# An attention-and-experts kernel on one core: each engine's instructions tied together in the order of the kernel's own plan

## The chip, the cores and the metric

The kernel runs on one core of a Trainium2 chip. A core has five engines with an instruction queue each: TensorE (PE) multiplies matrices, VectorE (DVE), ScalarE (ACT) and GpSimd (POOL) work elementwise, and SyncE (SP) issues loads. Sixteen DMA engines move data between the core's memory (SBUF, with PSUM as the target of matmuls) and HBM. The metric is the device time of one execution, in microseconds (us).

## The reference

The input x holds 4 batches of 11456 tokens with 128 features, in fp32. Attention through 32 inducing points comes first, then a mixture of 8 experts of which each token takes the one with the largest logit:

```
def mab(q, kv):
    s = scale * (q @ kv.transpose(0, 2, 1))
    s = s - s.max(-1, keepdims=True)
    a = np.exp(s)
    a /= a.sum(-1, keepdims=True) + 1e-09
    return a @ kv
h = mab(I, x)                # 32 inducing points attend to all tokens
x = mab(x, h)                # all tokens attend to the 32 results
...
logits = x @ w_gate          # 45824 tokens, 8 experts
expert_idx = np.argmax(logits, axis=1)
...                          # gate_w: softmax probability of that expert
    h = np.maximum(xe @ w1[e], 0.0)      # 128 -> 1024
    ye = h @ w2[e]                       # 1024 -> 128
    out[mask] = gate_w[mask, None] * ye
```

## The kernel before

A token's attention output is a weighted mean of 32 rows. If one expert takes all tokens of a batch and the sign of every hidden unit is the same for all 32 rows, the expert can be applied to these 32 rows (`h4`) instead of to the tokens. The main path does so; a test for each token, with a threshold `thr`, finds those for which it doesn't hold, and a second path after the main one computes them if there are any.

A batch is cut into 6 groups of 15 blocks of 32 tokens in 4 partition quarters (GW = 480 columns). Two functions and one between them add the work of a batch to a plan:

- `attend(b)` takes groups in pairs. A group's transposed tokens `xt` (960 KB) are loaded by SP. Scores with the inducing points `it_s` are four matmuls (L199). DVE takes their peak (L364), POOL parts it by quarters (`mq`, L367), PE spreads it (L376), DVE takes the lowest (L382), ACT makes the exponentials `e1t` (L386), DVE turns them (`e`, L394), and PE sums (L403) over the tokens by row, `xn`, which are loaded (L305) or turned on PE (L315) and copied (L325). DVE collects the sums in `hs` (L416).
- `induced(b)` makes the batch's 32 rows: `hs` is folded (L457, L458), divided in steps on DVE (L468 to L477), centred to `hc` (L486, L488); logits of the 32 rows on PE (L481, L482) give the expert by steps on DVE, the picking and the gate matrix `gzw` (L493 to L527). POOL gathers that expert's two weight matrices, `w1r` and `w2r`, by indirect DMAs (L510). Hidden units (L539 to L556), `h4` (L569, L579, L583, L587) and the threshold (L592 to L612) follow.
- `tokens(b, g0)` takes three groups: scores with `hc` (L199 again), the peak (L646 to L650), exponentials `et` on ACT (L654), gate logits on PE (L658), turned on DVE (L668), the gate in steps on DVE with one exponential on ACT (L675 to L708), its factors turned (`cb`, L715), `et` weighed by them on POOL (L718), the expert's rows by four matmuls into four PSUM banks `ps` (L722), four copies on ACT (L733), and a store that ACT issues (L736).

The order is made in two steps. Each of these operations is added to a `Plan` with its engine, an estimated duration, what it comes after, a rank, and the ring buffers it takes and gives back (12 of `xt`, 3 each of `xn`, `ob`, `e1t`, `e1`, `fe`, 8 `et`, 2 each of `lv` and `cb`, 1 `lp`, 4 `ps`). `Plan.order()` is a list scheduler: it starts whichever ready operation can start first by the estimates, the rank deciding between equals, and gives back the operations in the order of their planned starts. They are then written out in that order:

```
for op in plan.order():
    op["fn"]()
```

An operation may be several instructions. What is written out goes through the scheduler of the framework in which the kernel is written. This second scheduler keeps what depends on each other in order and is free to move the rest on each engine, by costs and priorities of its own. In the lists of instructions each engine's row differs from the plan's on PE, DVE, ACT and POOL, and not on SP's loads. An engine works through its row from the front.

## Time and profile before

| | |
|---|---|
| time, three runs | 231.03, 234.84, 235.23 us; median 234.84 |
| profiled execution | 233.27 us, of which the span of instructions is 231.5 |
| granted clock of PE, mean | 0.892 of 2.4 GHz |
| busy | PE 81%, DVE 57%, ACT 45%, POOL 17% |
| moved by DMA | 63.78 MB, 276 GB/s in the mean |

The span runs from the first to the last instruction of the profiled execution; the rest of its time lies around it. Shares are of the span. PE loads weights beside its matmuls, and a matmul's row may stand for several (xN) of one group. The granted clock is either near 1.00 or near 0.50 at a moment, so that a mean between them says how long each held.

### The profile page before, as it was taken

The numbers are of one execution on the slowest core, as the hardware profiler recorded it, in microseconds if no ns is written. First come the engines' busy times: TensorE is split into PE (matmuls) and PEld (weight loads), VectorE is DVE, ScalarE is ACT, GpSimd is POOL, SyncE is SP. The second block draws the span as 40 slices with busy tenths as digits, with TensorE's granted clock in tenths as the row PEclk, the third lists the DMA queues.
The fourth block names the chain that finished last, engine by engine and source line by source line (L and its number), as shares of the span: only waits on it lengthen the run. The fifth ranks groups of instructions, "written<-read, shape, count | busy, mean of one in ns | idle before, by whom it ended". The sixth has DMA issues, their size and how long they took to land.

```text
span 231.5 us, 4416 instructions
## 1 busy us (share of the span) xinstructions
PE 188.5 (81%) x1694; PEld 94.7 (41%) x1695; DVE 132.0 (57%) x400; ACT 104.7 (45%) x212; POOL 40.3 (17%) x58
## 2 busy tenths in 40 slices
PE   0897588898997799989999959999598959984840
PEld 0565364456665233544352236535122224422520
DVE  0275536674489266874894680848844998037300
ACT  2243204263350827385735841396236532845630
POOL 2000003000003500060045000410530062303200
PEclk9999889999999889999999997999959995578555
DMA  6999999995369847997999990034427524627591
GB/s 222 426 428 423 427 423 422 415 417 194 94 253 342 352 171 288 355 365 266 326 426 418 428 369 15 4 150 195 170 71 280 235 105 173 254 100 327 243 394 58
DMA packets 10252, 63.78 MB, mean 276 GB/s; under 512 B 1392, under 2 KB 1520, under 8 KB 10224
## 3 DMA queue, kind: packets, MB, share of 16 engines
q1 hardware_dynamic: 5328, 35.62, 39.2%
q10 hardware_dynamic: 3744, 23.62, 25.0%
q0 software_dynamic: 1152, 4.19, 4.8%
q8 instruction: 15, 0.25, 0.4%
q14 instruction: 13, 0.11, 0.1%
HBM read 39.83 MB, written 23.59 MB: 274 GB/s over the span
## 4 chain that ended last, share of the span: by engine, by line
PE 55%; DVE 19%; DMA 10%; ACT 6%; issue 3%; POOL 3%; SPq 0%; ACTq 0%; DVEq 0%; POOLq 0%
PE ps L722 16%; PE fe L199 15%; PE lp L658 8%; PE ps L403 8%; DMA xt<-in_xT 6%; PE ps L315 4%; DMA w1r<-in_w,ii 4%; ACT ob L733 3%; DVE cb L715 3%; POOL et L718 3%; DVE e L394 2%; DVE mx L364 2%; ACT e1t L386 2%; DVE mx L646 1%; ACT xn L325 1%
## 5 line engine op out<-in xcount | busy, mean ns | idle before, releaser
L733 ACT COPY ob<-ps 128x480 f32<-128x480 f32 x96 | 47.5, 573 | 34.0 <-PE ps L722 33.8
L722 PE MATMUL ps<-et,h 32*128 32x480 f32 x192 | 47.9, 739 | 10.3 <-POOL et L718 6.2
L718 POOL TENSOR_TENSOR et<-et,cb 128x480 f32<-128x480 f32 x24 | 28.4, 1211 | 56.2 <-DVE cb L715 36.8
L199 PE MATMUL fe<-xt,it_s 128*32 128x480 f32 x192 | 29.6, 609 | 9.7 <-DMA xt<-in_xT 9.7
L325 ACT COPY xn<-ps 128x512 f32<-128x512 f32 (+1 forms) x42 | 22.4, 570 | 26.1 <-PE ps L315 23.8
L364 DVE TENSOR_REDUCE mx<-fe 128x1 f32<-128x480 f32 x24 | 15.6, 652 | 27.9 <-PE fe L199 25.7
L722 PEld LDWEIGHTS ps<-et,h 32*128 32x128 f32 x192 | 17.6, 216 | 33.7 <-POOL et L718 13.8
L199 PE MATMUL fe<-xt,hc 128*32 128x480 f32 x192 | 29.4, 613 | 1.6 <-ACT e1t L386 1.1
L315 PE MATMUL ps<-csb,xt 128*128 128x128 f32 x180 | 27.1, 291 | 1.5 <-DMA xt<-in_xT 1.5
L658 PE MATMUL lp<-et,gzw 128*128 128x480 f32 x48 | 27.5, 661 | 0.5 <-ACT et L654 0.5
L654 ACT ACTIVATE et<-fe,rn 128x480 f32<-128x480 f32 x24 | 16.0, 671 | 26.1 <-DVE rn L650 16.6
L403 PE MATMUL ps<-xn,e 128*32 128x129 f32 x630 | 25.7, 282 | 1.7 <-DVE e L394 1.7
L315 PEld LDWEIGHTS ps<-csb,xt 128*128 128x128 f32 x180 | 21.7, 153 | 13.1 <-issue 6.2
L403 PEld LDWEIGHTS ps<-xn,e 128*32 128x32 f32 x630 | 21.8, 113 | 9.0 <-DVE e L394 2.5
L394 DVE STREAM_TRANSPOSE e<-e1t 128x480 f32<-128x480 f32 x24 | 15.1, 656 | 7.9 <-ACT e1t L386 7.8
L386 ACT ACTIVATE e1t<-fe,rn 128x480 f32<-128x480 f32 x24 | 14.8, 667 | 10.2 <-DVE rn L382 9.8
L646 DVE TENSOR_REDUCE mx<-fe 128x1 f32<-128x480 f32 x24 | 15.4, 643 | 6.1 <-PE fe L199 5.8
L715 DVE STREAM_TRANSPOSE cb<-c_all 128x480 f32<-128x480 f32 x24 | 15.4, 663 | 5.5 <-POOL et L718 5.0
L367 POOL TENSOR_TENSOR mq<-mx,csb 128x8 f32<-128x8 f32 x12 | 2.4, 201 | 91.3 <-DVE mx L364 91.2
L658 PEld LDWEIGHTS lp<-et,gzw 128*128 128x128 f32 x48 | 8.0, 207 | 13.5 <-issue 7.0
L668 DVE STREAM_TRANSPOSE lv<-lp 128x480 f32<-128x480 f32 x8 | 5.4, 671 | 14.3 <-PE lp L658 14.3
L199 PEld LDWEIGHTS fe<-xt,it_s 128*32 128x32 f32 x192 | 6.3, 113 | 16.0 <-issue 10.4
(94 smaller groups left out, 149.2 us busy)
## 6 DMA issues: line engine op xcount, KB each, us to landing
xt<-in_xT SPq DMA_DIRECT2D x24, 960.0 KB, 9.7
out<-ob ACTq DMA_DIRECT2D x24, 960.0 KB, 3.8
xn<-in_xn SPq DMA_DIRECT2D x9, 967.5 KB, 8.0
ob<-in_xn SPq DMA_DIRECT2D x3, 967.5 KB, 15.7
csb<-in_consts SPq DMA_DIRECT2D x1, 134.5 KB
w1r<-in_w,ii POOLq DMA_INDIRECT x4, 7.7
w2r<-in_w,ii POOLq DMA_INDIRECT x4, 9.3
it_sb<-in_indT ACTq DMA_DIRECT2D x1, 16.0 KB
```

Source lines behind the costliest of these rows:

```text
L199: nc.tensor.matmul(blk(ps[32 * q : 32 * q + 32, :GW]), lhsT=lhsT, rhs=xt_g[:, :, q, :], start=True, stop=True)
L315: nc.tensor.transpose(ps[:, k * P : (k + 1) * P], s.xt[g][:, k0 + k].rearrange("p q t -> p (q t)"), ident)
L325: nc.scalar.copy(dst, src)
L364: nc.vector.tensor_reduce(s.mx[:, g : g + 1], w.ps[:, :GW], AX.X, ALU.max)
L386: nc.scalar.activation(w.et, w.ps[:, :GW], AF.Exp, bias=pr.rn)
L394: nc.vector.transpose(w.e1, w.et)
L403: nc.tensor.matmul(hp[32 * j : 32 * j + 32, :], lhsT=blk(w.e1)[:, k, :], rhs=w.xn[:, k, :], start=(n < 4), stop=(n >= 2 * GB - 4),)
L658: nc.tensor.matmul(buf(some[0].b5)[:, :GW], lhsT=s.gzw[:, u * P : (u + 1) * P], rhs=w.et, start=(u == 0), stop=(u == NW - 1),)
L715: nc.vector.transpose(blk(w.cb), c.unsqueeze(2).to_broadcast([P, GB, 32]))
L718: nc.gpsimd.tensor_tensor(out=w.et, in0=w.et, in1=w.cb, op=ALU.mult)
L722: nc.tensor.matmul(buf(w.b9, q)[:, :GW], lhsT=s.h4[32 * q : 32 * q + 32, :], rhs=w.et[32 * q : 32 * q + 32, :], start=True, stop=True,)
L733: nc.scalar.copy(w.ob[:, q, :], buf(w.b9, q)[:, :GW])
```

## The change

After the operations are written out, the instructions of the main path are gone through in the order in which they were written, which is the plan's, and each gets a dependency on the one before it on the same engine. The dependency has no semaphore (`NoSync`): it sets the order for the framework's scheduler and adds no instruction and no wait on the chip.

```
     for op in plan.order():
         op["fn"]()
+    order = mybir.DependencyInfo(mybir.DependencyClass.NoSync, mybir.DependencyReason.DATA)
+    latest = {}
+    for ins in list(nc.cur_bb.bb.instructions):
+        if ins.engine in latest:
+            tc.add_manual_dep(ins, latest[ins.engine], order, reason="the plan's order")
+        latest[ins.engine] = ins.name
```

Below are the rows of instructions of some engines at the places that the prediction speaks of. A row gives the line, the operation, its output and inputs with their buffers (the number behind a ring's name is the buffer), and the shape; a first character of - or + says that it stands there only before or only after.

First place, PE, where the last of the loaded groups (`xt11`, of the last batch) gets its scores with the inducing points:

```order
-L658 MATMUL lp0_130<-et3_118,gzw1_136 128x480
 L603 MATMUL ps3_134<-dd_1410,ones_64 128x128
-L199 MATMUL fe2_129<-xt11_102,it_s_71 32x480
 L583 MATMUL ps1_132<-h1_1431,csb_60 128x128
 L315 MATMUL ps0_131<-csb_60,xt9_100 128x128 x3
+L658 MATMUL lp0_130<-et3_118,gzw1_136 128x480
 L403 MATMUL ps2_133<-xn1_104,e12_114 32x129 x15
-L199 MATMUL fe2_129<-xt11_102,it_s_71 32x480 x3
+L199 MATMUL fe2_129<-xt11_102,it_s_71 32x480 x4
 L403 MATMUL ps2_133<-xn2_105,e10_112 32x129 x15
```

The four score matmuls now stand together, behind L583, three transposes and fifteen sums, and one L658 has moved behind L603, L583 and the transposes.

The same place on DVE, before, from the peak of that group:

```order
L364 TENSOR_REDUCE mx_978<-fe2_129 128x1
L698 SCALAR_TENSOR_TENSOR rs_1465<-lm_1491,rs_1465 128x45
L704 TENSOR_REDUCE se_1501<-ex_1495 128x45
L416 SCALAR_TENSOR_TENSOR hs_981<-hs_981,fc_1364,ps2_133 128x129
L705 TENSOR_SCALAR se_1501<-se_1501 128x45
L706 RECIPROCAL se_1501<-se_1501 128x45
L708 TENSOR_TENSOR c_all_70<-se_1501,rs_1465 128x15x3
L715 STREAM_TRANSPOSE cb1_126<-c_all_70 128x480
L715 STREAM_TRANSPOSE cb0_125<-c_all_70 128x480
```

And after:

```order
L698 SCALAR_TENSOR_TENSOR rs_1465<-lm_1491,rs_1465 128x45
L704 TENSOR_REDUCE se_1501<-ex_1495 128x45
L705 TENSOR_SCALAR se_1501<-se_1501 128x45
L706 RECIPROCAL se_1501<-se_1501 128x45
L708 TENSOR_TENSOR c_all_70<-se_1501,rs_1465 128x15x3
L416 SCALAR_TENSOR_TENSOR hs_981<-hs_981,fc_1364,ps2_133 128x129
L715 STREAM_TRANSPOSE cb1_126<-c_all_70 128x480
L715 STREAM_TRANSPOSE cb0_125<-c_all_70 128x480
L364 TENSOR_REDUCE mx_978<-fe2_129 128x1
```

The peak of the last group has moved behind the gate's steps and two turned factors.

Second place, DVE, where `induced(3)` begins (`rv`, `hT_all`, `hb`, `hm`, `hc`) among the gate of three groups of batch 2 (`se`, `c_all`, `cb`). Before:

```order
L715 STREAM_TRANSPOSE cb0_125<-c_all_70 128x480
L468 TENSOR_SCALAR rv_1659<-ps1_132 128x32
L715 STREAM_TRANSPOSE cb1_126<-c_all_70 128x480
L469 RECIPROCAL rv_1659<-rv_1659 128x32
L715 STREAM_TRANSPOSE cb0_125<-c_all_70 128x480
L470 TENSOR_TENSOR hT_all_69<-rv_1659,ps1_132 128x128
L646 TENSOR_REDUCE mx2_1720<-fe1_128 128x1
L477 TENSOR_REDUCE hb_1663<-hT_all_69 128x1
L648 STREAM_TRANSPOSE mt_1722<-mx2_1720 128x32
L486 TENSOR_SCALAR hm_1668<-hb_1663 128x1
L650 TENSOR_REDUCE rn2_1724<-mt_1722 128x1
L488 TENSOR_SCALAR hc_1670<-hT_all_69,hm_1668 128x32
```

And after:

```order
L698 SCALAR_TENSOR_TENSOR rs_1640<-lm_1650,rs_1640 128x45
L468 TENSOR_SCALAR rv_1659<-ps1_132 128x32
L469 RECIPROCAL rv_1659<-rv_1659 128x32
L470 TENSOR_TENSOR hT_all_69<-rv_1659,ps1_132 128x128
L477 TENSOR_REDUCE hb_1663<-hT_all_69 128x1
L486 TENSOR_SCALAR hm_1668<-hb_1663 128x1
L488 TENSOR_SCALAR hc_1670<-hT_all_69,hm_1668 128x32
L704 TENSOR_REDUCE se_1676<-ex_1666 128x45
L705 TENSOR_SCALAR se_1676<-se_1676 128x45
L706 RECIPROCAL se_1676<-se_1676 128x45
L708 TENSOR_TENSOR c_all_70<-se_1676,rs_1640 128x15x3
L715 STREAM_TRANSPOSE cb0_125<-c_all_70 128x480
```

The six steps to `hc` stand in one block ahead of the end of the gate (L704 on) instead of one by one behind it. What follows in the new order is the picking and the gate matrix (L493 to L527, nine instructions), the other two L715, and then the peak L646 of `mx2_1720`.

The same place on POOL, where the weighing of the groups in `et4` to `et6` and the gathers of batch 3 meet:

```order
 L718 TENSOR_TENSOR et4_119<-et4_119,cb0_125 128x480
+L510 DMA w1r_1709<-in_w1,ii_1696 128x1024
+L510 DMA w2r_1710<-in_w2,ii_1696 128x1024
 L718 TENSOR_TENSOR et5_120<-et5_120,cb1_126 128x480
 L718 TENSOR_TENSOR et6_121<-et6_121,cb0_125 128x480
-L510 DMA w1r_1709<-in_w1,ii_1696 128x1024
-L510 DMA w2r_1710<-in_w2,ii_1696 128x1024
```

Both gathers have moved ahead of two of the three weighings.

Third place, POOL, where the gathers of batch 2 meet three weighings of batch 1:

```order
+L510 DMA w1r_1277<-in_w1,ii_1253 128x1024
+L510 DMA w2r_1278<-in_w2,ii_1253 128x1024
 L718 TENSOR_TENSOR et6_121<-et6_121,cb0_125 128x480
 L718 TENSOR_TENSOR et7_122<-et7_122,cb1_126 128x480
 L718 TENSOR_TENSOR et0_115<-et0_115,cb0_125 128x480
-L510 DMA w1r_1277<-in_w1,ii_1253 128x1024
-L510 DMA w2r_1278<-in_w2,ii_1253 128x1024
```

Here they have moved ahead of all three.

On ACT, a store stands directly behind the last of its group's four copies for 23 of 24 groups after, and for 8 of 24 before.

## Rows read from the trace of the kernel before

**Rows 1.** The page: busy time and share of each engine, with its instructions, and the chain of work that ended last, by engine.

```profile
PE 188.5 (81%) x1694; PEld 94.7 (41%) x1695; DVE 132.0 (57%) x400; ACT 104.7 (45%) x212; POOL 40.3 (17%) x58
...
PE 55%; DVE 19%; DMA 10%; ACT 6%; issue 3%; POOL 3%; SPq 0%; ACTq 0%; DVEq 0%; POOLq 0%
```

**Rows 2.** The table of stretches: from and to, length, busy us (and instructions) of PE, PE's weight loads, DVE, ACT and POOL, the mean granted clock, the share of the DMA engines and GB/s.

```profile
40.00:130.00 90.00, 82.69 (x894) 42.41 (x896) 58.42 (x178) 45.80 (x95) 16.05 (x22) 0.98 0.82 316
...
163.00:177.00 14.00, 10.83 (x40) 3.14 (x36) 8.26 (x30) 3.84 (x9) 5.43 (x5) 0.76 0.42 150
...
195.00:206.00 11.00, 11.00 (x28) 4.42 (x26) 1.47 (x3) 7.45 (x15) 3.51 (x3) 0.54 0.43 180
206.00:223.00 17.00, 11.87 (x42) 5.85 (x42) 8.47 (x20) 10.13 (x21) 3.61 (x3) 0.68 0.65 267
```

**Rows 3.** The timeline at the first place: start, duration, engine (SPq is SP's issue of a load), line, operation, output and inputs, shapes, and in brackets the idle time before it and what ended it.

```profile
131.02 0.33 SPq L356 DMA_DIRECT2D xt<-in_xT  x1
...
139.35 0.99 PE L199 MATMUL fe<-xt,it_s 128*32 128x480 f32 x2 [3.28 <-DMA xt<-in_xT]
...
143.69 0.83 PE L199 MATMUL fe<-xt,it_s 128*32 128x480 f32 x3
...
144.59 0.66 DVE L364 TENSOR_REDUCE mx<-fe 128x1 f32<-128x480 f32 x1 [5.77 <-PE fe L199]
...
145.16 0.20 DVE L698 SCALAR_TENSOR_TENSOR rs<-lm,rs 128x45 f32<-128x45 f32 x1
...
147.00 1.24 DVE L715 STREAM_TRANSPOSE cb<-c_all 128x480 f32<-128x480 f32 x2
...
147.83 2.37 POOL L718 TENSOR_TENSOR et<-et,cb 128x480 f32<-128x480 f32 x2 [2.30 <-DVE cb L715]
...
150.65 0.40 PE L376 MATMUL fe<-mq,csb 128*128 128x24 f32 x2
```

**Rows 4.** The timeline at the second place, same columns.

```profile
161.17 0.31 PE L458 MATMUL ps<-csb,hs 128*128 128x32 f32 x2
...
161.93 0.21 DVE L698 SCALAR_TENSOR_TENSOR rs<-lm,rs 128x45 f32<-128x45 f32 x1
...
162.29 1.01 PE L199 MATMUL fe<-xt,hc 128*32 128x480 f32 x8
...
163.74 0.68 DVE L715 STREAM_TRANSPOSE cb<-c_all 128x480 f32<-128x480 f32 x1
164.34 0.15 DVE L468 TENSOR_SCALAR rv<-ps 128x32 f32<-128x32 f32 x1
...
165.84 1.07 PE L722 MATMUL ps<-et,h 32*128 32x480 f32 x2 [2.53 <-POOL et L718]
...
167.62 0.51 DVE L488 TENSOR_SCALAR hc<-hT_all,hm 128x32 f32<-128x32 f32 x1
...
169.19 0.17 DVE L493 COPY gs<-ps 128x16 f32<-128x16 f32 x1 [1.06 <-PE ps L482]
...
170.49 0.98 POOL L510 DMA_INDIRECT w1r<-in_w,ii  x1 [2.39 <-DVE go L519]
...
170.98 3.43 PE L199 MATMUL fe<-xt,hc 128*32 128x480 f32 x16
170.99 0.27 DVE L527 TENSOR_TENSOR gzw<-csb,gz 128x108 f32<-128x108 f32 x1
...
171.78 0.94 POOL L510 DMA_INDIRECT w2r<-in_w,ii  x1 [0.30 <-issue]
...
174.34 1.15 PE L722 MATMUL ps<-et,h 32*128 32x480 f32 x8
...
177.12 1.07 PE L658 MATMUL lp<-et,gzw 128*128 128x480 f32 x2
```

**Rows 5.** The timeline of the end, same columns (ACTq is ACT's issue of a store).

```profile
203.78 2.58 PE L658 MATMUL lp<-et,gzw 128*128 128x480 f32 x4
...
206.40 0.68 DVE L668 STREAM_TRANSPOSE lv<-lp 128x480 f32<-128x480 f32 x1 [9.11 <-PE lp L658]
...
213.44 1.98 PE L722 MATMUL ps<-et,h 32*128 32x480 f32 x8 [2.98 <-POOL et L718]
...
222.76 0.34 ACTq L736 DMA_DIRECT2D out<-ob  x1
```

**Rows 6.** The timeline of DVE in one gate, same columns.

```profile
159.85 0.23 DVE L675 TENSOR_SCALAR rs<-lv 128x45 f32<-128x45 f32 x1
160.00 0.52 DVE L694 TENSOR_REDUCE lm<-lv 128x45 f32<-128x360 f32 x1
...
162.13 0.53 DVE L704 TENSOR_REDUCE se<-ex 128x45 f32<-128x360 f32 x1
...
162.70 0.19 DVE L705 TENSOR_SCALAR se<-se 128x45 f32<-128x45 f32 x1
```

**Rows 7.** The timeline of ACT around a store that stands directly behind its last copy, same columns.

```profile
128.85 0.34 ACTq L736 DMA_DIRECT2D out<-ob  x1
...
129.23 1.21 ACT L386 ACTIVATE e1t<-fe,rn 128x480 f32<-128x480 f32 x2 [0.42 <-ACT ob L733]
```

**Rows 8.** The timeline of POOL at the third place, same columns.

```profile
118.77 3.53 POOL L718 TENSOR_TENSOR et<-et,cb 128x480 f32<-128x480 f32 x3 [9.71 <-DVE cm L496]
...
122.59 0.98 POOL L510 DMA_INDIRECT w1r<-in_w,ii  x1 [0.29 <-DVE mt L648]
```

## The prediction

> **What bounds the kernel now.** I read the page's busy times and its chain first. They give the profiled execution a span of 231.5 us, with PE busy for 188.5 of it and PE holding 55% of the chain, DVE 19%, DMA 10% [rows 1]. An average of 81% hides different limits, so the second view was the table of stretches [rows 2]. From 40 to 130 us PE works 82.69 of 90.00 us at a granted clock of 0.98: whatever order the engines run in, at most 7.3 us can come out there. From 131 us on it is otherwise. From 163 to 177 PE works 10.83 of 14.00 at a mean clock of 0.76; from 195 to 206 it is busy all the time, but at 0.54, close to the lower of its two levels (1.2 GHz, where 1.00 is 2.4); from 206 to 223 it works 11.87 of 17.00. There PE stands or runs slowly because one chain of dependent steps is late, and an order can change that. Third, I read the timeline from 118 us to the end with the order of both kernels beside it, and walked each engine through its new row of instructions with the durations of the rows of before. Three places give the sum.
>
> **Term A, the last load of xt.** It is issued at 131.02, and its scores start at 139.35, after PE stood for 3.28 us [rows 3]. Before, the first of the four score matmuls of this group stands on PE ahead of L583, three transposes and fifteen sums of L403, and the other three behind them. So the scores end only at 143.69 + 0.83 = 144.52. On DVE their peak (L364) starts at 144.59 after 5.77 us of idling, and the gate's steps of the older tokens (L698 onward) stand behind it although they don't need it; the turned factors (L715) come at 147.00, the weighing at 147.83, and the spread of the peaks (L376) at 150.65 [rows 3]. In the new order L583, the transposes, one L658 and L403 stand ahead of all four score matmuls, so they run inside the wait, and the scores run as one piece. At full clock one group's scores take 1.01 us [rows 4]: they would end at 140.36, 4.2 us earlier. At the low level two groups take 3.43 [rows 4], so one takes 1.7: end at 141.1, 3.4 earlier. On DVE the gate's steps and two L715 now stand ahead of L364. Against this, the L658 that moved behind L603, L583 and the transposes runs about 2 us later, and so do the gate's steps that follow from it: factors at about 143 instead of 147.00. The spread then waits for a POOL that has two weighings of about 1.2 us (2.37 for two [rows 3]) ahead of it: about 146.5 instead of 150.65. Gain 1.5 (if the later L658 governs) to 4.2; I take 3.0, near the 3.28 that PE stood, since PE is what is short right after.
>
> **Term B, the induced points of batch 3.** The matmuls L457 and L458 end at 161.48, but DVE reaches the first of the six steps to hc (L468) at 164.34 and the last (L488) at 167.62, each step having another instruction of the gate between it and the next. PE waits 2.53 us for the weighing at 165.84, the scores with hc start at 170.98, the experts of the next group at 174.34, and L658 at 177.12 [rows 4]. In the new order the six steps stand in one block behind L698, which ends at 162.14 [rows 4]. Their durations, first 0.15 and last 0.51, add to 1.49 (six rows); with 0.04 between dependent steps, hc is there at 163.9. Scores of two groups at full clock: 164.0 to 166.0. The gate's end is L704 to the start of L715, 1.61 us from 162.13 to 163.74 [rows 4, 6]; started at 163.9 it gives factors at 165.4 and a first L715 (0.68) by 166.1, a weighing by 167.3, experts by 168.4. Then DVE has the picking of the expert, 169.19 to 171.26, 2.07 us [rows 4], ahead of the second L715, done at 168.9. POOL has both gathers, 170.49 to 172.72, 2.23 us [rows 4], ahead of the second weighing, which ends at 170.8. The second experts end at 171.9, and L658 follows: 5.2 us before 177.12. In this walk PE still stands 1.3 and 2.4 us, after which its clock may stay low, and I was generous with hops: range 0.5 to 5.2, taken 3.5.
>
> **Term C, from there to the last L658.** Before, from 177.12 to 203.78 + 2.58 = 206.36 is 29.2 us [rows 4, 5]. The walk through the new order gives 26 to 26.7, mostly because the chain from the gathers to the expert's folded rows ends earlier and eviction, weighing and scores meet fewer waits. But in the new order the peak of a group (L646) stands behind a whole gate chain with its L715, its exponential comes some 3 us late on ACT, and four evictions stand behind that. Range -2 to 3.5, taken 2.0. From the last L658 on, the gate (206.40), the three weighings and experts (213.44) and the last store (222.76) are one chain [rows 5] whose order is the same in both but for the stores: nothing.
>
> **The stores.** ACT issues each store, and in the new order 23 of 24 stand directly behind their last copy, before 8. The row where it stood so shows the price: issue at 128.85, and the next activation starts at 129.23 with 0.42 us idle behind the copy [rows 7]. 15 more of these are 6.3 us of ACT; but ACT is busy 104.7 of 231.5 us [rows 1] and mostly waits, so this counts only where evictions hold banks that PE waits for. Range 0 to 2 us lost, taken 0.5. The Trainium skill ("DMA: Bandwidth & Descriptors", "Issuing engines are not separate DMA queues") says that the time which initiating a DMA costs on the issuing engine is usually small. By that the term would be nothing and the sum 0.5 more; the 0.42 idle of this trace is two thirds of one 128x480 activation, so I keep the row.
>
> **Steps no longer braided.** Before, independent instructions alternate on DVE; the new order puts dependent ones back to back. An independent step starts at 160.00 while its forerunner ends at 160.08, so 0.08 before the end; a dependent one starts at 162.70 after 162.13 + 0.53 = 162.66, 0.04 behind it [rows 6]. That is 0.12 per step; the five links to hc lose 0.6, which the walk of term B contains. The Trainium skill ("VectorE: DVE Perf Modes", "The DRAIN you can't avoid") has it that the next DVE operation doesn't start until the pipe is empty, whether or not a wait stands between. By it braiding would have brought nothing, and B would be 0.6 more. The trace differs, by the 0.08 of the row at 160.00, and the row counts.
>
> **Elsewhere, 40 to 130 us.** PE has at most 7.3 us to give [rows 2]. The walk gave 2 to 4 up to 116 us, and then a new wait of about as much at the place of the first rival. Zero, from -4 to +4.
>
> **Sum.** 3.0 + 3.5 + 2.0 - 0.5 = 8.0. The profiled execution took 233.27 (span 231.5 and 1.77 around it), 0.7% under the median of 234.84 and between the fastest and the slowest run. 233.27 - 8.0 = 225.3, and the three runs spread by 1.8%, so 2%, 4.7 us, is about what a measurement tells from no change.
>
> **The rivals.** *First, the hold-up inside batch 2 eats term A.* In the order before, three weighings run at 118.77 and the gathers follow at 122.59 [rows 8]. In the new order the picking (2.07 on DVE) and the gathers (2.23 on POOL) stand ahead of the first of these weighings, 4.3 us together [rows 4]; the experts behind them on PE hold up the scores that free the buffer of the last xt, whose load left at 131.02. If this load leaves 4.3 later, the 3.0 of term A go, and another 1.3. For it: xt is the load on which PE waits at 139.35. Against: PE has other work there, and part of the gathers' 2.23 falls beside the picking's last steps. 225.3 + 4.3 = 229.6, within 2%. *Second, slower: the same hold-up in batches 1 and 2, with PE slow after each.* Without term A the rest of the sum is 5.0. Each hold-up costs 4.3, and behind each PE falls to its low level, as from 195 to 206 [rows 2], for 4 us of work that would take 2 at full clock: 2 more. 233.27 - 5.0 + 2 x 6.3 = 240.9. It decides from 4.8 per place on. For it: loads are late in batch 1 as well, and a wait of one instruction now stops all that stand behind it on its engine. [...] *Third, the gain comes out whole*, with the front: 4.2 + 5.2 + 3.5 + 3.0 = 15.9, 217.4. For it: every end of the walks comes from rows; against: PE's clock and the ring buffers that I carried by hand.
>
> **How the numbers follow.** The forecast (225.3, own range 220 to 228.6) gets 0.48; the whole gain 0.10; the first rival 0.25; the slower one 0.17. The range reaches from 217.4, the third rival, to 238, beyond the 237.9 at which slower begins, and leaves out most of the second rival and little else. Faster by over 2% 0.58, within 2% 0.25, slower 0.17.
>
> **What would show it.** For A: the scores of the last xt in one piece, within 2 us of its landing, and L376 of that pair some 4 us earlier. For B: L488 within 2.5 us of L458, the scores with hc right after. For C: less than 28 us from L658 of that group to the last one, and a clock above 0.54 in the stretch that answers to 195 to 206. For the first rival: PE idle of 3 us or more ahead of L722 where the first gathers of a batch are issued, and a last load of xt issued after 133. The prediction is wrong if PE's idle time before 130 grows, since the walk there was the longest and its result the least sure.

## The result and the profile after

The changed kernel takes 221.48 us in the median of four executions (219.37 to 222.55), the kernel before 234.81 in the same comparison (231.03 to 235.23). The ratio is 0.9491, with a 95% interval of 0.9417 to 0.9564: faster by 5%. The forecast was 225.3. Executions of one kernel lie a few us apart, with different granted clocks; the ratios here leave out executions more than 1.5% above the kernel's fastest, the medians take all.

The profiled execution of after is its slowest of the four: 222.55 us, span 220.7. Against the profiled execution before (233.27, span 231.5) the span is 10.8 shorter. The page's busy times, with each engine's share of the span and its instructions, and the chain of work that ended last, by engine:

```profile
PE 175.5 (80%) x1694; PEld 87.7 (40%) x1695; DVE 138.4 (63%) x400; ACT 105.5 (48%) x212; POOL 40.1 (18%) x58
...
PE 40%; DVE 26%; DMA 13%; ACT 9%; issue 4%; POOL 4%; ACTq 1%; DVEq 0%; POOLq 0%
```

Read this beside [rows 1], and subtract before anything else. The page counts 4423 instructions in all, 7 more than before; the 7 are semaphore instructions of PE and ACT, so that "adds no instruction" holds only for those that compute. PE runs the same 1694 matmuls in 175.5 us instead of 188.5: 13.0 less, which is more than the span lost. PE's idle time did not shrink. It was 231.5 - 188.5 = 43.0 and is 220.7 - 175.5 = 45.2. So the order did not take waiting away from PE in sum. It made PE's own work shorter, and the clock is no reason for that in sum, since its mean fell from 0.892 to 0.878. The page's groups say which work (busy, mean ns of one, idle before it and what ended that). First before, then after:

```profile
L722 PE MATMUL ps<-et,h 32*128 32x480 f32 x192 | 47.9, 739 | 10.3 <-POOL et L718 6.2
```

```profile
L722 PE MATMUL ps<-et,h 32*128 32x480 f32 x192 | 37.6, 741 | 13.7 <-POOL et L718 12.2
```

The experts' matmuls alone account for 10.3 of the 13.0, with the same number of them and the same duration of one. Together they can take less only if more of them run beside each other. The timeline shows how. An expert's group is four matmuls on four quarters of 32 rows (eight records, two for each). In the order before, one such group stands on PE in three pieces, with L583 and the scores of another group between them:

```profile
88.77 1.07 PE L722 MATMUL ps<-et,h 32*128 32x480 f32 x4
...
90.19 1.07 PE L722 MATMUL ps<-et,h 32*128 32x480 f32 x2
...
92.13 1.07 PE L722 MATMUL ps<-et,h 32*128 32x480 f32 x2
93.13 1.07 PE L658 MATMUL lp<-et,gzw 128*128 128x480 f32 x2
```

And the same work after:

```profile
86.84 1.09 PE L722 MATMUL ps<-et,h 32*128 32x480 f32 x8
87.86 1.07 PE L658 MATMUL lp<-et,gzw 128*128 128x480 f32 x2
```

Whole, the group holds PE for 87.86 - 86.84 = 1.02 us. Torn, each piece holds it for 1.00, however few matmuls are in it, and the group takes 3.0. The Trainium skill ("TensorEngine Tiling (Array Packing)", "Key Properties") says that different tiles of the array can run matmuls in parallel. The trace agrees for tiles that stand next to each other in the row of instructions, and shows the price where other work stands between them: 1.0 per piece at full clock, 1.9 at the low level. Before, three of the 24 groups are torn by other work, into 3, 4 and 2 pieces, and two by a wait inside them (those that start at 121.20 and 174.35); after, none is. The table of stretches for L722 alone (from and to, length, busy us and instructions of PE and of its weight loads, clock, DMA) gives the one in four pieces with its neighbour at place B, before and then after:

```profile
165.00:178.00 13.00, 6.72 (x16) 1.75 (x16) 0.74 0.44 156
```

```profile
162.00:170.00 8.00, 3.07 (x16) 0.83 (x16) 0.79 0.54 195
```

The 10.3 us of L722 are then these: 6.72 - 3.07 = 3.65 here, 3.21 - 1.09 = 2.1 at the group shown first, 7.46 - 4.25 = 3.2 at place C, and 2.53 - 1.17 = 1.4 at the first group of all. Not all of it is tearing. At C the clock was 0.50 before and is 1.00 after; two whole groups at the low level take 5.93 at the end of before (216.15 to 222.08), so that by estimate 1.5 of the 3.2 is the tearing and 1.7 the clock. The first group was whole and at full clock in both: before, its four matmuls came some 0.4 apart behind ACT's copies (L325). That leaves, by estimate, 7 of the 10.3 for torn groups.

The table of stretches after (columns as in [rows 2]):

```profile
40.00:130.00 90.00, 78.68 (x894) 40.54 (x898) 61.49 (x180) 47.87 (x97) 16.62 (x23) 0.94 0.85 326
...
185.00:196.00 11.00, 8.43 (x31) 3.02 (x28) 6.35 (x17) 6.45 (x13) 3.50 (x3) 0.69 0.44 182
```

From 40 to 130 PE completes 894 matmuls in both. It needs 78.68 us for them instead of 82.69, and idles the 4.0 that this saves (11.3 instead of 7.3): the front gained work time and lost it again to waiting. The stretch that answers to 195 to 206 of before is 185 to 196 now, at 0.69 instead of 0.54.

By the prediction's own marks the 10.8 are made up as follows (negative is earlier after):

| stretch, with the marks that end it | before | after | difference | taken |
|---|---|---|---|---|
| start to L539 of batch 2 | 131.13 | 130.78 | -0.35 | 0 |
| A: to the fifth L668 (start) | 28.00 | 24.13 | -3.87 | -3.0 |
| B: from there to L658 of `et1` (177.12, now 169.06) | 17.99 | 14.15 | -3.84 | -3.5 |
| C: from there to the end of the last L658 | 29.24 | 26.44 | -2.80 | -2.0 |
| the end of the span | 25.14 | 25.20 | +0.06 | +0.5 (stores) |

The median moved by 13.3 and the two profiled spans by 10.8, because the profiled execution of before lies 1.5 under its median and that of after 1.1 above its own.

The three places after, from the timeline. First place A, to be read beside [rows 3]:

```profile
130.68 0.33 SPq L356 DMA_DIRECT2D xt<-in_xT  x1
...
137.25 0.59 PE L199 MATMUL fe<-xt,it_s 128*32 128x480 f32 x1
137.45 0.98 PE L199 MATMUL fe<-xt,it_s 128*32 128x480 f32 x7
...
142.03 2.36 POOL L718 TENSOR_TENSOR et<-et,cb 128x480 f32<-128x480 f32 x2 [15.73 <-DVE cb L715]
...
144.60 0.40 PE L376 MATMUL fe<-mq,csb 128*128 128x24 f32 x2
```

The scores are one piece from 137.25 to 138.43 (144.52 before), the weighing starts 5.8 earlier and the spread of the peaks 6.05 earlier. Place B, beside [rows 4]:

```profile
156.95 0.31 PE L458 MATMUL ps<-csb,hs 128*128 128x32 f32 x2
...
159.17 0.24 DVE L488 TENSOR_SCALAR hc<-hT_all,hm 128x32 f32<-128x32 f32 x1
159.56 1.82 PE L199 MATMUL fe<-xt,hc 128*32 128x480 f32 x16
...
163.02 1.09 PE L722 MATMUL ps<-et,h 32*128 32x480 f32 x8 [1.65 <-POOL et L718]
...
167.15 1.98 PE L722 MATMUL ps<-et,h 32*128 32x480 f32 x8 [3.05 <-POOL et L718]
169.06 1.97 PE L658 MATMUL lp<-et,gzw 128*128 128x480 f32 x2
```

`hc` is there 159.41 - 157.26 = 2.15 us behind the end of L458, where it was 168.13 - 161.48 = 6.65, and the scores with it follow at once. PE then stands 1.65 and 3.05 (the walk had 1.3 and 2.4). Third, POOL and PE where the gathers of batch 2 stand, beside [rows 8]:

```profile
116.09 0.98 POOL L510 DMA_INDIRECT w1r<-in_w,ii  x1 [10.18 <-DVE go L519]
...
118.34 3.50 POOL L718 TENSOR_TENSOR et<-et,cb 128x480 f32<-128x480 f32 x3
...
119.59 1.98 PE L722 MATMUL ps<-et,h 32*128 32x480 f32 x8 [3.11 <-POOL et L718]
121.50 1.97 PE L658 MATMUL lp<-et,gzw 128*128 128x480 f32 x2
123.40 1.83 PE L199 MATMUL fe<-xt,it_s 128*32 128x480 f32 x8
```

This is the hold-up of the first rival: both gathers ahead of the weighings, PE standing 3.11 us for the first of these, and three groups of matmuls behind it at the low level. It is where the front gives back what it gained: the gathers leave 6.5 us earlier than before (116.09 against 122.59), the weighings only 0.4 (118.34 against 118.77).

### The profile page after: what moved, and what is told of

It is laid out like the page before. It is cut to its first block, busy times and chain, and to the rows that moved or that the text cites. A ratio compares the mean times of both kernels' runs of the same rounds, so it can differ in the third digit from the quotient of the medians.

```text
span 220.7 us, 4423 instructions
## 1 busy us (share of the span) xinstructions
PE 175.5 (80%) x1694; PEld 87.7 (40%) x1695; DVE 138.4 (63%) x400; ACT 105.5 (48%) x212; POOL 40.1 (18%) x58
## 4 chain that ended last, share of the span: by engine, by line
PE 40%; DVE 26%; DMA 13%; ACT 9%; issue 4%; POOL 4%; ACTq 1%; DVEq 0%; POOLq 0%
PE fe L199 11%; DMA xt<-in_xT 10%; PE ps L722 9%; PE lp L658 8%; PE ps L403 6%; ACT ob L733 5%; DVE cb L715 4%; POOL et L718 3%; PE ps L315 3%; DMA wg_sb<-in_wg 2%; ACT e1t L386 2%; DVE mx L646 2%; DVE lv L668 1%; DVE ls L679 1%; DVE e L394 1%
## 5 line engine op out<-in xcount | busy, mean ns | idle before, releaser
L733 ACT COPY ob<-ps 128x480 f32<-128x480 f32 x96 | 46.6, 574 | 26.1 <-PE ps L722 26.1
L722 PE MATMUL ps<-et,h 32*128 32x480 f32 x192 | 37.6, 741 | 13.7 <-POOL et L718 12.2
L199 PE MATMUL fe<-xt,it_s 128*32 128x480 f32 x192 | 28.5, 646 | 9.2 <-DMA xt<-in_xT 7.7
L325 ACT COPY xn<-ps 128x512 f32<-128x512 f32 (+1 forms) x42 | 22.1, 569 | 28.6 <-PE ps L315 28.3
L658 PE MATMUL lp<-et,gzw 128*128 128x480 f32 x48 | 29.7, 709 | 5.2 <-ACT et L654 5.1
L364 DVE TENSOR_REDUCE mx<-fe 128x1 f32<-128x480 f32 x24 | 15.5, 645 | 22.3 <-PE fe L199 22.3
L722 PEld LDWEIGHTS ps<-et,h 32*128 32x128 f32 x192 | 14.4, 224 | 33.2 <-POOL et L718 19.7
L199 PE MATMUL fe<-xt,hc 128*32 128x480 f32 x192 | 26.4, 611 | 1.0 <-ACT e1t L386 1.0
L315 PE MATMUL ps<-csb,xt 128*128 128x128 f32 x180 | 26.0, 284 | 1.4 <-DMA xt<-in_xT 1.4
L403 PEld LDWEIGHTS ps<-xn,e 128*32 128x32 f32 x630 | 19.9, 110 | 8.7 <-issue 2.9
L403 PE MATMUL ps<-xn,e 128*32 128x129 f32 x630 | 22.8, 274 | 0.4 <-DVE e L394 0.4
L646 DVE TENSOR_REDUCE mx<-fe 128x1 f32<-128x480 f32 x24 | 15.3, 638 | 8.0 <-ACT e1t L386 4.0
L715 DVE STREAM_TRANSPOSE cb<-c_all 128x480 f32<-128x480 f32 x24 | 15.4, 662 | 1.6 <-POOL et L718 1.1
L658 PEld LDWEIGHTS lp<-et,gzw 128*128 128x128 f32 x48 | 8.5, 219 | 19.8 <-ACT et L654 14.6
L199 PEld LDWEIGHTS fe<-xt,it_s 128*32 128x32 f32 x192 | 5.0, 113 | 14.9 <-issue 9.9
L668 DVE STREAM_TRANSPOSE lv<-lp 128x480 f32<-128x480 f32 x8 | 5.3, 667 | 8.2 <-PE lp L658 8.2
```

The source lines that it names most:

```text
L199: nc.tensor.matmul(blk(ps[32 * q : 32 * q + 32, :GW]), lhsT=lhsT, rhs=xt_g[:, :, q, :], start=True, stop=True)
L315: nc.tensor.transpose(ps[:, k * P : (k + 1) * P], s.xt[g][:, k0 + k].rearrange("p q t -> p (q t)"), ident)
L325: nc.scalar.copy(dst, src)
L403: nc.tensor.matmul(hp[32 * j : 32 * j + 32, :], lhsT=blk(w.e1)[:, k, :], rhs=w.xn[:, k, :], start=(n < 4), stop=(n >= 2 * GB - 4),)
L646: nc.vector.tensor_reduce(m, w.ps[:, :GW], AX.X, ALU.max)
L658: nc.tensor.matmul(buf(some[0].b5)[:, :GW], lhsT=s.gzw[:, u * P : (u + 1) * P], rhs=w.et, start=(u == 0), stop=(u == NW - 1),)
```

## The experiments

Each kernel below is the changed one with another row of instructions, and nothing is left out of the computation. The changed kernel ties all instructions of the main path in the order of a list. In the experiments this list (`row`) is altered before it is tied; `made[n]` are the instructions of the plan's operation n, and `put(what, before)` moves instructions in the list. What an edit leaves untied, the framework's scheduler places. Distances in the text are from the start of a mark to the start of the next: front (to L539 of batch 2), A (to the fifth L668), B (to the sixth), C (to the last). By these the kernel before has 131.13, 28.00, 19.10 and 28.17, after 130.78, 24.13, 16.16 and 24.47.

### Half of the change

```
+    first = row.index(made[448][0])
+    row[:] = row[:first]
```

Operation 448 is L539 of batch 2. This kernel, front_only, ties only what lies ahead of it; back_only has `row[first:]` in the second line and ties only what lies behind.

> The instructions are tied in the plan's order only up to the first use of the gathered rows of batch 2 (PE's L539, at 131 us in both kernels); behind that the framework orders them itself. My theory: up to there the plan's order gains 4.8 us by 116 us and gives back all but 0.3 where the weighing waits for picking and gathers, so alone it is worth nothing: ratio to the kernel before 0.99 to 1.00. The rival, that the front carries the change (loads leave earlier, and later waits shrink because of it), expects 0.97 or less. A third, that the hold-up at 117 to 120 us costs more once the rest doesn't follow the plan, expects 1.01 or more.

> The other half: the framework's own order up to the first use of the gathered rows of batch 2 (131 us), the plan's order from there on. My theory, that the gain lies behind the last loads (terms A, B and C of the prediction), expects nearly the whole gain, some 10 us: ratio to the kernel before 0.950 to 0.960. The rival, that half of it comes from the front, expects 0.97 to 0.98.

With the tie in front only: 224.77 us, ratio 0.9578 (0.948 to 0.9676). With the tie behind only: 224.02, ratio 0.9576 (0.9498 to 0.9654). So the back half works as expected (A 23.46, B 16.16, C 25.13), and my expectation of almost nothing from the front half was wrong. In its trace the front ends at 127.69 instead of 131.13, C takes 26.56 instead of 28.17, and A, untied, takes 23.25, because the second scheduler, coming from another state, also puts the four scores of the last xt in one piece there:

```profile
133.58 1.01 PE L199 MATMUL fe<-xt,it_s 128*32 128x480 f32 x8 [0.92 <-DMA xt<-in_xT]
```

Its B is that of before (19.18). So both halves hold the gain of A, and their gains can't be added.

back_only also shows what A is worth by the order alone. Its last load of xt is issued at 131.63, 0.1 ahead of L539 as before, and takes 8.3 us as before; the scores start as one piece, 8.2 behind that L539:

```profile
139.93 1.01 PE L199 MATMUL fe<-xt,it_s 128*32 128x480 f32 x8 [1.34 <-DMA xt<-in_xT]
```

And yet its A takes 23.46 where the kernel before takes 28.00. PE's clock was 1.00 in that stretch and 0.94 before, which has a small part in the 4.5.

### One place undone

In undo_a:

```
+    put(made[610][:1], made[453][0])
+    put(made[611], made[335][2])
```

In undo_b:

```
+    six = made[624] + made[626]
+    braid = made[475] + six[:1] + made[484] + six[1:2] + made[493] + six[2:3]
+    for peak, step in zip(made[511], six[3:]):
+        braid += [peak, step]
+    put(braid, made[627][0])
+    put(made[628], made[520][0])
+    put(made[477][:1], made[625][0])
+    put(made[477][1:2], made[625][1])
+    put(made[477][2:3], made[640][0])
```

The first restores at place A the order of before: one score matmul ahead of L583, and the peak L364 ahead of the gate's steps. The second restores place B: on DVE the six steps L468 to L488 one by one among three L715 and L646 to L650, on POOL the gathers behind three weighings, on PE three matmuls of L722 around L481 and L482.

> All tied as in the change, but at the last loaded group the first of its four score matmuls stands again ahead of L583 on PE, and its peak L364 again ahead of the gate's L698 on DVE. In the changed kernel that load lands at 136.5 us instead of 139.3, so the wait is shorter. Theory 1, that term A was the order: the loss is the 3.0 us of the prediction, in the trace a PE wait of 1.5 us or more at L199 and the spread L376 3 us later; ratio to before 0.960 to 0.965. Theory 2, that more than half of the gain there was the earlier landing: the order is worth 1 to 2 us, ratio 0.953 to 0.958. Theory 3, that the earlier landing alone did it: no loss, 0.949.

> All tied as in the change, but where batch 3's induced points begin the three engines stand as before: on DVE the six steps to hc one by one behind the gate's end, on POOL the gathers behind all three weighings, on PE three experts' matmuls ahead of the scores. My theory (term B): 2.9 to 3.5 us are lost, ratio to before 0.961 to 0.964. The rival, that what is lost there is given back in the waits for POOL that the change has there (1.65 and 3.05 us at L722), expects 0 to 1 us: 0.949 to 0.953. The walk's own end, 5.2 us, would be 0.971.

undo_a takes 224.8 us, 3.3 more than after in the median. Its ratio, 0.9543 (0.946 to 0.9627), lies only 0.005 above that of after, 1.2 us, and the intervals overlap: the time alone doesn't tell the loss from none, nor the theories from each other. The trace, of its longest execution (227.1 us), shows the loss at its place. A takes 30.89 instead of 24.13, since the lone score matmul stands on PE and waits:

```profile
136.30 1.81 PE L199 MATMUL fe<-xt,it_s 128*32 128x480 f32 x2 [4.02 <-DMA xt<-in_xT]
```

The 6.8 is more than the order alone: this load was issued at 127.72 and took 8.5 us where it took 5.8 after, and PE's mean clock from 127.65 to 141.12 was 0.76.

undo_b takes 226.2 us of 235.04, by medians 0.9624 (after 0.9432, 4.5 us less); a ratio for it isn't on record. That is more than the rival's 0 to 1 us. Its B takes 21.66 instead of 16.16, with PE's mean clock at 0.76 in that stretch, 0.86 after and 0.82 before, so that the clock has a part in the 5.5. Its rows of PE show the torn group beside the late `hc`:

```profile
159.03 1.55 PE L722 MATMUL ps<-et,h 32*128 32x480 f32 x2 [3.42 <-POOL et L718]
...
161.04 1.96 PE L722 MATMUL ps<-et,h 32*128 32x480 f32 x2
...
163.46 1.96 PE L722 MATMUL ps<-et,h 32*128 32x480 f32 x2
165.35 3.43 PE L199 MATMUL fe<-xt,hc 128*32 128x480 f32 x16
...
170.91 1.07 PE L722 MATMUL ps<-et,h 32*128 32x480 f32 x2 [0.64 <-ACT ob L733]
```

The four pieces hold PE for 1.48 + 1.89 + 1.89 + 1.08 = 6.3 us, where the whole group holds it for 1.9 at the low level. `hc` was there at 161.32 (L488 at 160.81, 0.51 long), but its scores start at 165.35, because two more pieces stand ahead of them. So place B is worth what the table of the result gives it. For A the table's 3.9 stands beside the 4.5 of back_only; undo_a gives the sign and not the size.

undo_a also separates the clock from the order in front of it. Its rows up to L539 of batch 2 are those of after, and the wait is the same:

```profile
119.33 1.09 PE L722 MATMUL ps<-et,h 32*128 32x480 f32 x8 [3.11 <-POOL et L718]
```

Here the group behind the wait takes 1.09 where it took 1.98, and the stretches from 111 to 125 are, after and undo_a:

```profile
111.00:125.00 14.00, 10.89 (x110) 4.90 (x109) 9.68 (x35) 5.90 (x12) 5.42 (x5) 0.78 1.01 406
```

```profile
111.00:125.00 14.00, 10.83 (x125) 5.56 (x121) 10.28 (x35) 7.29 (x15) 5.63 (x6) 1.00 1.01 423
```

From that L722 to L539 after needs 11.19 us, undo_a 8.32: 2.9 us by the clock alone, with the same instructions. undo_b and front_only lie between (9.91, 9.93), late3 below is like after (11.29). So the clock fell behind this wait in four traces of the five, in two of them before the first group behind it, and held in one. In these five executions of one order L539 starts anywhere from 127.18 to 130.78.

### The hold-ups moved

In late2:

```
+    put(made[445] + made[447], made[570][0])
+    put(made[446], made[586][0])
```

In late3:

```
+    put(made[627] + made[629], made[511][0])
+    put(made[628], made[520][0])
```

late2 puts the picking, the gate matrix and the gathers of batch 2 behind the factors and the weighings of batch 1; late3 does so for batch 3, at place B; late23 has all four lines.

> As the change, but in batch 2 the picking and the gate matrix (L493 to L527, on DVE) stand behind the first two L715, and the two gathers (on POOL) behind all three weighings. In the changed kernel PE waits 3.11 us there for the first weighing and works at its low level behind it. Theory 1, that this hold-up eats what the front gains: the wait goes, PE's clock stays up, and the kernel is 2.5 to 4 us faster than the change: ratio to before 0.931 to 0.940. Theory 2, that the gathers, issued some 3 us later, then hold L539: what is gained comes back as a wait there, at most 1 us is left: 0.945 to 0.950. Theory 3, that a fall of the clock alone is what differs between executions: the slow executions go, the fastest stays at 219: 0.937 to 0.942.

> The same move in batch 3 alone: picking and gate matrix behind all three L715, gathers behind all three weighings. The changed kernel has a wait of 3.05 us there at the second experts (L722) and L722, L658 and L199 at the low level behind it. Theory 1: 2.5 to 4 us faster than the change, ratio to before 0.931 to 0.940. Theory 2, that the evictions on ACT (each group's four copies take 1.95 us) would hold the second experts anyway: 1 us or less, 0.945 to 0.950. That gathers come too late is not expected: they land at 171.9 us and are used at 177.

> Both moves together. If each removes a wait on the path by itself, their gains add: 5 to 8 us faster than the change, ratio to before 0.915 to 0.928. If one place only passes the wait on to the next, the sum is no more than the larger of the two: 0.930 to 0.940.

late2: 220.71 us, ratio 0.9424 (0.9381 to 0.9468). The wait of 3.11 is gone, in its place stand one of 0.64 ahead of the first six matmuls, 1.27 ahead of the other two (the group is torn again, by a wait for DVE's L414) and 1.28 ahead of L658. The clock falls all the same, and the front ends at 129.98: 0.8 less, which is inside the spread of one order. The ratio lies just above the range of the third theory and inside none, and its interval reaches all three. So moving the picking behind the factors doesn't remove the wait: it goes over to the next results that DVE then makes late.

late3: 220.85 us in the median of eight executions (216.28 to 222.64), by medians 0.9429 of before. Its ratio, 0.9253 (0.9189 to 0.9317), rests on three of them, and no execution lies between 217.31 and 220.63; so how much it gains on the change, from next to nothing by the medians to 5.6 us by the ratios, stays open. In the profile its B shrinks from 16.16 to 14.44, both weighings being ready for one run of two whole groups:

```profile
161.89 4.17 PE L722 MATMUL ps<-et,h 32*128 32x480 f32 x16 [1.65 <-POOL et L718]
```

late23: 219.15 us, ratio 0.9371 (0.9323 to 0.9418), in the range of the second theory: the two gains don't add. B takes 15.28 there, the front 128.96.

### The stores untied

```
+    row[:] = [i for i in row if i.name not in stores]
```

`stores` holds the names of the 24 instructions of L736.

> As the change, but the 24 stores are left out of the tie, so that the framework places them among ACT's instructions as it did before; all else keeps the plan's order. The prediction's term: a store directly behind its last copy idles ACT for 0.42 us, and 0.5 us of the whole is lost by it: ratio to before 0.946 to 0.948. The bound above: 2 us, 0.941. The page's rule as the prediction read it (an issue costs the engine next to nothing): no difference, 0.949.

218.81 us, ratio 0.9257 (0.9196 to 0.9318), faster than all three expected. The framework's scheduler puts 20 of the 24 stores one instruction later, behind the next activation or the next group's first copy; 4 stay directly behind their last copy. ACT after, with the store directly behind its last copy:

```profile
98.69 1.94 ACT L733 COPY ob<-ps 128x480 f32<-128x480 f32 x4
100.66 0.34 ACTq L736 DMA_DIRECT2D out<-ob  x1
101.04 0.29 ACT L390 ACTIVATE fc<-rn 128x1 f32<-128x1 f32 x1 [0.42 <-ACT ob L733]
```

And with the stores untied:

```profile
96.57 1.94 ACT L733 COPY ob<-ps 128x480 f32<-128x480 f32 x4
98.36 0.34 ACT L390 ACTIVATE fc<-rn 128x1 f32<-128x1 f32 x1
98.54 0.34 ACTq L736 DMA_DIRECT2D out<-ob  x1
```

The 0.42 us of idling are gone. By medians the stores cost 221.48 - 218.81 = 2.7 us (2.1 with the two medians of the kernel before, 234.81 and 234.23, set equal). The ratios would give 5.5, but that of stores_free rests on three of its six executions. In the profile the front ends at 125.75 with the stores untied; the fastest of the five traces with the stores tied, undo_b, has 127.18 at the same mean clock (0.97), 1.4 more.

### One engine's row alone

```
     for ins in list(nc.cur_bb.bb.instructions):
+        if not str(ins.engine).endswith("PE"):
+            continue
```

This is only_pe; only_dve has "DVE" there.

> Only PE's instructions are tied in the plan's order (its row is then the change's); DVE, ACT and POOL are ordered by the framework. The halves of the kernel each gave 4.2%, so the question is which engine's row carries it. Theory 1, PE's row: the score matmuls of the last load no longer split and the experts' matmuls no longer ahead of the logits; 5 us or more of the 13 come, ratio to before 0.96 to 0.98. Theory 2, that DVE's row decides (the steps to hc and the gate stay braided here): 0.98 to 1.00. Theory 3: a plan's order on one engine among the framework's on the others puts its instructions behind results that come late, slower: 1.01 or more.

> Only DVE's instructions are tied in the plan's order; PE, ACT and POOL are ordered by the framework (POOL's row comes out as in the change all the same). Theory 1, PE's row carries the gain: 0.98 to 1.00. Theory 2, DVE's row does: 0.96 to 0.97, with hc of batch 3 within 3 us of L458. Theory 3, the mixture is slower: 1.01 or more.

PE's row alone: 221.06 us, ratio 0.9378 (0.931 to 0.9445), more than the first theory expected and as much as the whole change, whose interval overlaps. The front ends at 125.49, A takes 24.73; B doesn't gain (19.84), although its group is whole, since DVE's six steps are late again:

```profile
157.91 0.36 PE L481 MATMUL ps<-wg_sb,hT_all 128*128 128x8 f32 x2 [3.51 <-DVE hT_all L470]
```

DVE's row alone: 232.96 us in the median of seven executions from 227.27 to 239.15, by medians 0.9914. Its ratio, 0.9714 (0.9624 to 0.9804), rests on the three shortest, and its interval crosses 2%: whether this row alone gains is unclear. In the trace, of an execution of 232.96, B (16.29) and A (24.29) gain, but the front ends at 141.13, 10 us later than before. PE's untied row tears two groups there (into 3 and 2 pieces), and the hold-up at the gathers is still there; but PE's mean clock up to that mark was 0.92 instead of 0.97, so that how much of the 10 the order costs stays open. B takes DVE's row, and PE's row alone brings the gain in the front; A, and C too (25.14 and 24.42), came with either.

### The best order found

stores_late3 joins the untied stores with late3. stores_late23b also treats batch 2, with the picking behind only one L715 and the gate matrix later, so that no wait tears the group:

```
+    put(made[445][:1], made[570][0])
+    put(made[445][1:] + made[447], made[325][0])
+    put(made[446], made[586][0])
+    put(made[627] + made[629], made[511][0])
+    put(made[628], made[520][0])
+    row[:] = [i for i in row if i.name not in stores]
```

> The change with the stores left out of the tie, and in batch 3 picking, gate matrix and gathers behind the factors and weighings. Each alone gave a median of 219 to 221 us with a fastest execution of 216, against 221.5 and 219.4 of the change. If the two are separate places on the path, they add: median 216 to 218, ratio to before 0.92 to 0.93. If the stores' gain ahead of 131 us only meets a later wait that the other move had already removed: no better than one of them, 0.935 to 0.94.

> The same, and in batch 2 the picking (but for the copy of its logits) and the gate matrix behind the collecting of the sums (L414), one peak of each kind and the third L715, and the gathers behind all three weighings. With the picking only behind two L715 the wait of 3.11 us went over into one of 1.27 for L414 and one of 1.28 for an exponential, both late because DVE was still picking. If that was the whole of it, PE's clock now stays up from 116 to 125 us and 2 to 3 us more go: ratio 0.91 to 0.92. If the gathers, then issued after 118 us, are late for L539: no better than without this move.

stores_late3: 218.05 us, ratio 0.9296 (0.9239 to 0.9353), where the sum of the two gains was expected; but the intervals of stores_free and late3 alone overlap it, so that adding isn't shown. stores_late23b: 216.29 us, ratio 0.9195 (0.9125 to 0.9265), the lowest median of all, in the range expected. Against the changed kernel that is 2.4% less, each taken against the kernel before of its own comparison (216.29 of 234.99, 221.48 of 234.81). Its hold-up in batch 2 is gone, and the clock holds where after has 0.81:

```profile
113.94 1.30 PE L722 MATMUL ps<-et,h 32*128 32x480 f32 x8 [0.23 <-POOL et L718]
...
113.00:131.00 18.00, 13.88 (x130) 5.96 (x122) 13.17 (x40) 10.96 (x23) 5.41 (x6) 1.00 1.01 400
```

The first group of experts starts there 5.65 us earlier than after (119.59). Whether it beats stores_late3 is not settled: they lie 0.8% apart, and their executions overlap (215.24 to 220.85 and 217.22 to 219.47).

## Why the prediction was right, and where it was not

**What bounds the kernel.** "PE stands or runs slowly because one chain of dependent steps is late, and an order can change that" names only half. PE's idle time grew by 2.2, and what shrank by 13.0 is its work. The premise that fails with it is "whatever order the engines run in, at most 7.3 us can come out there": busy time of PE was taken as fixed work, and from 40 to 130 the same 894 matmuls needed 4.0 less of it. Up to L539 of batch 2 PE is busy for 110.85 us before, 104.28 in stores_free and 107.35 in only_pe: all of the 5.4 by which the first's front is earlier, and 3.5 of the 5.6 of the second's. The walks were made with rows of whole groups ("scores of two groups at full clock", the x8 rows of L722), so the price of the torn ones came into the terms without being named. That is why the sizes hold better than the reason.

**Term A: right, at the upper part of its range.** 3.9 against 3.0 (1.5 to 4.2). The scores run as one piece, the sums inside the wait, the gate's steps ahead of the peak. "L376 of that pair some 4 us earlier" came out at 6.05. One part was not foreseen: the load that was issued 0.3 earlier landed about 2.8 earlier (139.3 before, 136.5 after, by 8.3 and 5.8 us from issue to landing). What goes with it in the traces is whether the second gather of batch 2 had landed when the load was issued. In the eight where it had, the load took 5.6 to 6.4 us; in the six where it was still under way (before, back_only, late2, undo_a, only_pe, stores_late23b) it took 7.4 to 9.7. That is an order of things; no run changed it alone. Term A doesn't rest on it: in back_only the load takes 8.3 as before, and A still gains 4.5.

**Term B: right.** 3.84 against 3.5; 5.5 in the trace of undo_b, at a lower clock, with 5.2 as the upper end. `hc` within 2.15 of L458, as the walk had it, and the 0.04 between dependent steps on DVE holds in after, where L468 ends at 158.01 and L469 starts at 158.05. The prediction found its trace at odds with the Trainium skill there. But the section of the Trainium skill that it cites ("VectorE: DVE Perf Modes", "The DRAIN you can't avoid") goes on that a next operation that isn't held starts earlier, and the 0.08 of [rows 6] agrees with that. The prediction gave the whole term to the chain on DVE and the queue on POOL. The trace of before shows a second part: `hc` was there at 168.13, and its scores started at 170.98 because a piece of a torn group ran until then. only_pe shows that a whole group without early steps brings nothing; early steps with a torn group weren't run, so the two shares stay open.

**Term C: right in sign, 2.8 against 2.0.** Two rows give the parts. Before, PE stands 1.83 us for the threshold's chain (L603 waits for L599) between L569 and the scores, which start at 190.84, 2.86 behind the start of L569 at 187.98. After, the distance is 0.99 (180.32 to 181.31): 1.9 us. And a group that is torn, at the low level, is whole after. Before:

```profile
191.92 1.96 PE L722 MATMUL ps<-et,h 32*128 32x480 f32 x2
...
194.54 5.50 PE L722 MATMUL ps<-et,h 32*128 32x480 f32 x14
199.97 1.97 PE L658 MATMUL lp<-et,gzw 128*128 128x480 f32 x2
```

After:

```profile
182.67 4.25 PE L722 MATMUL ps<-et,h 32*128 32x480 f32 x16
...
189.49 1.97 PE L658 MATMUL lp<-et,gzw 128*128 128x480 f32 x2 [2.57 <-ACT et L654]
```

From the first of these to L658 it takes 8.05 before and 6.82 after, 1.2 less. The 16 matmuls take 3.2 less (PE's clock is 0.50 there before and 1.00 after, and the after's two groups are paced by ACT's copies), L583 stands elsewhere, and 2.57 are lost to a wait for the exponential. That is the late exponential on ACT of which the term's lower bound was made.

**The stores: mis-sized.** Taken 0.5, range 0 to 2; by medians they cost 2.1 to 2.7 of the change's own gain. The price of one, 0.42 us on ACT, is as the row gave it. The Trainium skill's sentence ("DMA: Bandwidth & Descriptors", "Issuing engines are not separate DMA queues") reads "usually small relative to the DMA itself". The trace agrees, with 0.42 against 3.7 us from issue to landing of a store; by that the term is small beside a DMA, and that it would be nothing is the prediction's own reading. The step that failed is "this counts only where evictions hold banks that PE waits for", judged by ACT's busy share of the whole span [rows 1]. What the runs show is a front that ends 1.4 us earlier at the same clock with the stores untied; that the 0.42 is a step in the chain from a group's exponential to the next weighing is argued from the rows.

**Elsewhere: zero came out by luck.** The walk's "2 to 4 up to 116 us, and then a new wait of about as much" is what happened, 3.11 us at the place named. But the prediction's own last sign of being wrong came as well: PE's idle time from 40 to 130 grew, from 7.3 to 11.3 us. The sum held because PE's work shrank by 4.0 there, for which the prediction had no term. And the result depends on the clock behind the wait: -0.35 in the profile of after, -3.95 in that of undo_b, at the same order.

**The first rival** has its wait and its place right, and its consequence wrong. The load of the last xt left at 130.68, not after 133; the front's gain paid for the hold-up and term A stayed. **The slower rival** rightly had PE's clock fall behind a wait of about 3 us in the front (3.11 to 3.41 in the traces). The clock fell in four of the five traces of that order, and cost 2.9 us between after and undo_a; but the wait came in one batch and not in two, and the earlier gain stood against it. **The whole gain with the front** (217.4) is about what the best of the orders reached, 216.29 with the hold-ups moved and the stores untied; the change itself did not.

## What to carry to other kernels

Read PE's busy time as something an order can change: where four matmuls on quarters of the array are one step, look whether they stand together in the instruction list, since each piece of a torn group costs as much as the whole one (1.00 against 1.02 us here), and no view of waits shows it. Fixing the order of that one engine gave the whole gain here. On the other engines, look whether what releases the busy engine (factors, weighings, evictions) stands ahead of what it needs only later (picking, gathers, stores): moving the stores gave 2 to 3 us by medians; what moving picking and gathers gives by itself stayed open. Before adding the gains of two halves of a change, see whether one place, here A, is in both.

## What the runs showed of the hardware

With the same instructions and the same 3.11 us wait, PE's granted clock fell in one execution and stayed at 1.00 in another (0.78 against 1.00 from 111 to 125), worth 2.9 us by the next mark. What decides between the two was not found. A load of 960 KB took 5.6 to 6.4 us from issue to landing in the eight traces in which an indirect gather ahead of it had landed before it was issued, and 7.4 to 9.7 in the six in which the gather was still under way.
